# Streaming attention and a GELU layer in one kernel: weight transfers back to back, values of block 1 on SyncE, bias on block 0

## Chip, cores and metric

The kernel runs on one core of a Trainium2 chip. Its time is device microseconds; the number compared is the median of several executions. Beside it there is one profiled execution, from which the page and the trace come.

## What is computed

Four batches, eight heads, 768 tokens, head dimension 64. Attention with a causal window of 128 tokens and four sink tokens that are always seen; its output, put back to 3072 rows of 512, goes through x·w_in (512 by 2048), a quick GELU and ·w_out (2048 by 512).

```python
keep = is_sink | in_window                       # pos < 4, or 0 <= row - column < 128
scores = np.where(keep, scale * q @ k.T, -1e9)
a = exp(scores - max) / (sum + 1e-9)
x = (a @ v).transpose(0, 2, 1, 3).reshape(3072, 512)
h = x @ w_in
out = (h / (1 + exp(-1.702 * h))) @ w_out
```

## The kernel before

The work is cut into twelve blocks of 256 tokens (NK = 12; block k is batch k // 3, part r = k % 3), each with four pairs of heads. A block goes through these stages:

- **Load** (function `load`): q, k and v of the block in float32, on SyncE's DMA queue (SP); the first k is on ScalarE's. Blocks 0 to 3 load q and k in two halves each (KT = 4). In the kernel before, v of block 1 alone is loaded by GpSimd (POOL). Three buffers (RS) hold the float32 data.
- **Cast** to float16 (recorded at line 277, the line of a helper): on POOL, for the first two blocks on VectorE (DVE), ScalarE (ACT) and POOL, as the planner places them.
- **Turn**: q and k are transposed into blkT, by TensorE (PE, line 504, then a copy) for blocks 0 to 3, by DMA transposes on SP from block 4.
- **Scores** (function `scores`): matmuls (line 586) and exp on ACT (line 606). What the window hides is taken away in one of two ways. For k < KM, bias matmuls on PE (line 579: bias times identity, accumulated ahead of the scores) put a large negative number there before the exp. For k >= KM, a multiply by a 0/1 mask on DVE follows the exp (line 613). KM is 2 before.
- **Sinks** (line 544, exp at 552) for blocks with r > 0; then the product with v (line 646), the division (664, 666), and the transpose to xT (685 and 692 for the first three blocks, a DMA transpose on SP later).
- **mm1** (line 713): eight groups of 8 matmuls per block, each followed by tanh on ACT (725) and a multiply on DVE (727) into gT. At most three groups are open (RTH = 3). w_in is cut into chunks w0 to w3, each of which serves two groups.
- **mm2** (line 741): 32 matmuls of 512 columns per block, 16 for each of its two row tiles, with chunk w4 + s // 2 of the weights for group s; scaling on ACT (759), stores on SP (773).

mm1 of block k - 1 and mm2 of block k - 2 run among the attention work of block k. The weights arrive as eight transfers that cast to float16 on the way (function `weights`, line 348), all issued by POOL, whose instruction stream they share with the casts.

**What sets the order.** A planner written in the kernel (`Plan.run`) places every operation on an engine at a modelled time, with costs, ends and buffers; the instruction order on each engine is the order of these times. `o.end` of a DMA is its modelled landing. The 700 ns of SLACK are added for DMA transposes alone. All loads and weights are also put in one list by priority and each must be planned after the one before it (`behind`). On top of that, from the tenth on, each gets a real wait on an earlier transfer ("gates"): the one some 3.8 us of transfer ahead of it (4.5 for those that POOL issues), so that few transfers are in flight at once. The order of the list is a0, a1, w0, w1, w2, w3, w4, a2, w5, w6, w7, where a2 stands for q, k and v of block 2 and w4 is the first chunk of w_out.

Of the kernel before, what the change touches and what calls it, by code (L numbers as in the profile page):

```python
# [33 lines left out]
class Op:  # L34
    def __init__(self, engs, fn, deps, prio, acq, rel, kind):

        self.engs, self.fn = engs, fn
        self.deps = [d for d in dict.fromkeys(deps) if d is not None]
        self.prio, self.acq, self.rel, self.kind = prio, acq, rel, kind
        self.eng = self.start = self.end = self.banks = self.places = self.behind = None  # L40
        self.users = []


HOP = {
    ("PE", "ACT"): 60, ("PE", "DVE"): 60, ("ACT", "DVE"): 60, ("DVE", "PE"): 80, ("ACT", "PE"): 80,
    ("DVE", "ACT"): 60, ("POOL", "PE"): 100, ("POOL", "DVE"): 100,
}
RING, LANES, SLACK = 163, 8, 700
ENGINES = ("PE", "ACT", "DVE", "POOL", "SP")


class Plan:
# [4 lines left out]
    def op(self, eng, dur, lat, fn, deps=(), prio=0.0, acq=None, rel=(), kind=""):  # L57
        return self.any({eng: (dur, lat)}, lambda _: fn(), deps, prio, acq, rel, kind)
# [8 lines left out]
    def run(self, warm=None, warm_until=0.0, late_bank=0.0):  # L67
# [4 lines left out]
        free = {e: 0.0 for e in ENGINES}  # L72
# [12 lines left out]
        def after(d, e):  # L85
            if d.eng != e or isinstance(d.engs[e][1], tuple):
                return d.end + HOP.get((d.eng, e), 50)
            return d.start + d.engs[e][0] + (0 if d.eng == "PE" else 60)

        def could(o, e):  # L90

            if o.behind and o.behind.start is None:
                return None, None
            s = max([free[e]] + [after(d, e) for d in o.deps])
            line = landed[e == "POOL"]
            if isinstance(o.engs[e][1], tuple) and len(line) >= LANES:
                s = max(s, line[-LANES])
            if not o.acq:
                return s, s
            cls, n = o.acq  # L100
            times = sorted(bank_free.values())
            places = sorted(count[cls].values())
            if len(times) < n or len(places) < n:
                return s, None
            return s, max(s, times[n - 1], places[n - 1])

        while todo:
            best = None
            for e in ENGINES:
                found = sorted(  # L110
                    [(*could(o, e), o) for o in ready[e]], key=lambda x: (x[2].prio, x[2].seq)
                )
                keep, held_from = [], None
                for s0, s, o in found:
                    if s0 is None:
                        continue
                    if o.acq and o.acq[1] > 2 and (s is None or s > s0):

                        held_from = s0 if held_from is None else min(held_from, s0)
                        if s is not None:  # L120
                            keep.append((s, o))
                        continue
                    if s is None or (o.acq and held_from is not None and s >= held_from):
                        continue
                    keep.append((s, o))
                if not keep:
                    continue
                first = min(s for s, _ in keep)
                s, o = min(((s, o) for s, o in keep if s <= first + 20), key=lambda x: (x[1].prio, x[1].seq))
                lat = o.engs[e][1]  # L130
                key = s if len(o.engs) == 1 else s + lat - min(x[1] for x in o.engs.values())
                if best is None or key < best[0]:
                    best = (key, s, o, e)
            if best is None:
                raise RuntimeError("no operation can be planned")
            _, s, o, e = best
            dur, lat = o.engs[e]
            if e == "PE" and warm and s < warm_until:
                t = max(free["PE"], 400.0)
                while t + 110 < s:  # L140
                    order.append((t, -1, warm, e, None))
                    t += 60
            for x in o.engs:
                ready[x].remove(o)
            o.eng, o.start = e, s
            if o.acq:
                cls, n = o.acq
                o.banks, o.places = [], []
                for _ in range(n):
                    b = min((b for b in bank_free if bank_free[b] <= s), key=lambda b: (bank_free[b], b))  # L150
                    del bank_free[b]
                    o.banks.append(b)
                    p = min((p for p in count[cls] if count[cls][p] <= s), key=lambda p: (count[cls][p], p))
                    del count[cls][p]
                    o.places.append(p)
            free[e] = s + dur
            if isinstance(lat, tuple):
                ns, nd = lat
                t = s + dur
                while sum(n * min(1.0, (b - t) / max(b - a, 1.0)) for a, b, n in ring[e] if b > t) + nd > RING:  # L160
                    t += 25
                free[e] = t
                soft = e == "POOL"
                begin = max(s + (2200 if soft else 1300), dma_free[soft])
                shared = max(0.0, min(dma_free[not soft] - begin, ns))
                if shared:
                    dma_free[not soft] += shared
                dma_free[soft] = begin + ns + shared
                ring[e].append((begin, dma_free[soft], nd))
                landed[soft].append(dma_free[soft] + 900)  # L170
                o.end = dma_free[soft] + 900 + (SLACK if o.kind in ("turn", "xturn") else 0)
            else:
                o.end = s + lat
            for owner, i in o.rel:
                t = o.end + 80
                bank_free[owner.banks[i]] = t
                count[owner.acq[0]][owner.places[i]] = t
            for u in o.users:
                u.left -= 1
                if not u.left:  # L180
                    for x in u.engs:
                        ready[x].append(u)
            order.append((s, o.seq, o.fn, e, o))
            todo -= 1
# [9 lines left out]
def kernel(  # L194
# [11 lines left out]
    nc = tc.nc  # L206
# [11 lines left out]
    scale = float(1.0 / np.sqrt(Dh))  # L218
    PAIRED_FROM, RR = 2, 3
    KT, KX, AHEAD = globals().get('OPT',{}).get('KT',4), 3, globals().get('OPT',{}).get('AHEAD',0)  # L220
    RB, KM, HIDE = 4, globals().get('OPT',{}).get('KM',2), 60000.0
    RS, RQ, RV, RA, RX, RG, RTH, RO = 3, 2, 4, 6, 3, 5, 3, 3

    pool = ctx.enter_context(tc.tile_pool(name="sb", bufs=1))
# [116 lines left out]
    def weights(j, at):  # L341
        if j < 4:
            src = moe_w_in[:, bass.ts(j, 512)].rearrange("(c p) f -> p c f", p=P)
            to = w_in16[:, :, bass.ts(j, 512)]
        else:
            src = moe_w_out[bass.ts(j - 4, 512), :].rearrange("(c p) f -> p c f", p=P)
            to = w_out16[:, 4 * (j - 4) : 4 * (j - 4) + 4]
        o_w[j] = op("POOL", 780, (2800, 33), lambda: nc.gpsimd.dma_start(to, src), prio=at, kind="w")  # L348
        loads.append(o_w[j])

    L = OPT.get('L',17300.0)
# [2 lines left out]
    def load_at(x):  # L354
        return NEVER + 10 * LOADS.index(x) + 3 if x in LOADS else 10000.0 + (int(x[1:]) - 3) * L
# [17 lines left out]
    def load(k):  # L373
# [7 lines left out]
        for e, src in enumerate((q, k_ap)):  # L381
# [10 lines left out]
            else:  # L392
                def f(e=e, src=src, dma=dma):
                    return dma.dma_start(dst[:, e], src[b, :, t0 : t0 + TB].rearrange("h (p i) d -> p h i d", i=2))
                lq[e].append(op(eng, 450, (1850, 64), f, war, prio=prio + e / 2, kind="load"))
            loads.extend(lq[e])
            if k == 1:
                o_first.extend(lq[e])
        def lv(dma, h):
            return lambda: dma.dma_start(dv[:, h], v[b, h, t0 : t0 + TB].rearrange("h (p i) d -> p h i d", i=2))  # L400

        soft = k == 1
        o_lv = [op("POOL" if soft else "SP", 1000 if soft else 450, (1850, 64), lv(nc.gpsimd if soft else nc.sync, slice(0, 8)),
                   war, prio=load_at("w0") + 5 if soft else load_at("a1") + 1.5 if k == 0 else prio + 0.7, kind="load")]

        loads.append(o_lv[0])

        c16 = qk16[k % RQ]
# [391 lines left out]
    for a_, b_ in zip(loads, loads[1:]):  # L800
        b_.behind = a_
    for n, o in enumerate(loads):
        if 9 <= n < 4 + 5 * KT + 8:
            m, ahead = n - 1, 0.0
            while ahead < (4500 if "POOL" in o.engs else 3800):
                ahead += next(iter(loads[m].engs.values()))[1][0]
                m -= 1
            g = o_first[1] if o is o_w[0] else loads[m]
            o.deps.append(g)
            gates.append((o, g))  # L810

    warm_bank = bank[6]

    def warm(_):
        nc.tensor.matmul(warm_bank[:, 0:P], zero, zero, start=True, stop=True)  # L815

    order = plan.run(warm=warm, warm_until=12000.0, late_bank=12500.0)
    with tc.manual_schedule():
# [42 lines left out]
```

## Time and profile before

| | us |
|---|---|
| median of 5 runs | 227.02 |
| lowest and highest run | 226.24, 229.21 |
| profiled execution | 228.77 |
| span of its instructions | 226.8 |

Busy time and share of the span by engine: PE 218.6 us (96%), DVE 126.0 (56%), ACT 132.6 (58%), POOL 91.0 (40%). The mean granted clock of TensorE is 0.996 of full speed. HBM is read at 27.36 MB and written at 6.29 MB over the span.

All times inside the profile count from the start of the span. A timeline row gives start, duration, engine, line and operation, the operands and the count of instructions that are merged; in brackets stands the idle time of the engine just before it and what ended that. A row of the waits gives the total, the number and the longest wait. A row of the chain gives start and length of a piece. "DMA qk<-in_q_dram" is the load of q. In the rows on DMA queues, q1 is SP's, q10 ACT's, q0 POOL's; the numbers are packets, MB, and the time that the packets took as a share of 16 engines' span.

### The profile page before, as it was taken

The numbers are of one execution on the slowest core, as the hardware profiler recorded it, in microseconds if no ns is written. First come the engines' busy times: TensorE is split into PE (matmuls) and PEld (weight loads), VectorE is DVE, ScalarE is ACT, GpSimd is POOL, SyncE is SP. The second block draws the span as 40 slices with busy tenths as digits, with TensorE's granted clock in tenths as the row PEclk, the third lists the DMA queues.
The fourth block names the chain that finished last, engine by engine and source line by source line (L and its number), as shares of the span: only waits on it lengthen the run. The fifth ranks groups of instructions, "written<-read, shape, count | busy, mean of one in ns | idle before, by whom it ended". The sixth has DMA issues, their size and how long they took to land.

```text
span 226.8 us, 5442 instructions
## 1 busy us (share of the span) xinstructions
PE 218.6 (96%) x2170; PEld 153.4 (68%) x2170; DVE 126.0 (56%) x274; ACT 132.6 (58%) x262; POOL 91.0 (40%) x158
## 2 busy tenths in 40 slices
PE   8999989989999999999999999999999999999991
PEld 8968867576766766766766766766676676766640
DVE  1585856667744855665565655665555655633400
ACT  3298546576647865655576676565476476444310
POOL 8296056068993594906609709209200000000000
PEclk9999999999999999999999999999999999999998
DMA  5999999998978989599596786986812312230232
GB/s 189 317 197 169 221 242 160 289 288 240 269 142 163 259 165 260 122 188 285 111 230 176 140 211 160 142 208 165 165 24 47 65 30 46 65 71 5 49 74 64
DMA packets 64808, 36.36 MB, mean 160 GB/s; under 512 B 27760, under 2 KB 59520, under 8 KB 64784
## 3 DMA queue, kind: packets, MB, share of 16 engines
q1 hardware_dynamic: 60000, 30.55, 56.6%
q0 software_dynamic: 4416, 4.82, 13.3%
q10 hardware_dynamic: 368, 0.66, 1.0%
q8 instruction: 17, 0.28, 0.5%
q14 instruction: 7, 0.06, 0.1%
HBM read 27.36 MB, written 6.29 MB: 148 GB/s over the span
## 4 chain that ended last, share of the span: by engine, by line
PE 81%; DMA 12%; POOL 4%; DVE 1%; issue 0%; ACT 0%; POOLq 0%
PE bank L741 34%; PE bank L713 32%; PE bank L646 5%; DMA w_out<-in_moe_w_out_dram 5%; PE bank L586 4%; DMA w_in<-in_moe_w_in_dram 3%; PE bank L815 3%; DMA qk<-in_q_dram 3%; PE bank L544 1%; POOL qk L277 1%; POOL vs L452 1%; PE bank L504 1%; POOL w_out L348 1%; DVE blkT L277 0%; POOL v L400 0%
## 5 line engine op out<-in xcount | busy, mean ns | idle before, releaser
L713 PE MATMUL bank<-xT,w_in 128*128 128x256 f16 x768 | 101.3, 273 | 0.0
L741 PE MATMUL bank<-w_out,gT 128*128 128x512 f16 x384 | 99.6, 379 | 1.3 <-DMA w_out<-in_moe_w_out_dram 1.3
L727 DVE SCALAR_TENSOR_TENSOR gT<-th,bank 128x512 f16<-128x512 f16 x96 | 65.7, 684 | 44.9 <-ACT th L725 43.8
L713 PEld LDWEIGHTS <-w_in 128*128 128x128 f16 x768 | 72.4, 98 | 22.7 <-issue 2.7
L725 ACT ACTIVATE th<-bank 128x512 f16<-128x512 f32 x96 | 57.7, 601 | 44.5 <-PE bank L713 42.7
L277 POOL CAST qk<-qk 64x512 f16<-64x512 f32 (+1 forms) x72 | 43.9, 610 | 57.5 <-DMA qk<-in_q_dram 48.8
L606 ACT ACTIVATE at<-bank 128x512 f16<-128x512 f32 (+1 forms) x96 | 50.4, 571 | 14.9 <-PE bank L586 14.6
L741 PEld LDWEIGHTS <-gT 128*128 128x128 f16 x384 | 35.7, 98 | 24.9 <-issue 2.1
L613 DVE TENSOR_TENSOR at<-at,bank 128x1024 f16<-128x1024 f16 (+1 forms) x40 | 25.6, 639 | 20.8 <-ACT at L606 20.8
L277 POOL CAST v<-v 64x512 f16<-64x512 f32 x45 | 27.6, 612 | 3.4 <-DMA v<-in_v_dram 1.1
L646 PE MATMUL bank<-v,at 128*128 128x65 f16 x352 | 21.1, 193 | 0.2 <-DVE v L277 0.2
L759 ACT ACTIVATE osb<-bank 128x512 f32<-128x512 f32 (+1 forms) x24 | 14.2, 591 | 11.8 <-PE bank L741 11.8
L646 PEld LDWEIGHTS <-at 128*128 128x128 f16 x352 | 17.6, 97 | 3.7 <-issue 0.2
L552 ACT ACTIVATE ats<-bank 128x256 f16<-128x256 f32 x32 | 12.5, 391 | 7.9 <-PE bank L544 7.9
L666 DVE TENSOR_TENSOR xb<-bank,rcp 128x256 f16<-128x256 f32 x36 | 15.1, 421 | 0.5
L646 PE MATMUL bank<-vs,ats 128*128 128x65 f16 x128 | 14.8, 193 | 0.0
L664 DVE RECIPROCAL rcp<-bank 128x4 f32<-128x4 f32 x48 | 8.6, 179 | 10.3 <-PE bank L646 9.8
L586 PE MATMUL bank<-blkT 64*128 64x256 f16 x192 | 13.4, 244 | 0.0
L586 PEld LDWEIGHTS <-blkT 64*128 64x128 f16 x256 | 8.0, 94 | 7.7 <-issue 6.2
L646 PEld LDWEIGHTS <-ats 128*128 128x128 f16 x128 | 12.0, 97 | 1.9 <-ACT th L725 0.2
L815 PE MATMUL bank<-zero 128*128 128x128 f16 x99 | 8.9, 268 | 1.0 <-DVE zero L290 1.0
L277 ACT COPY blkT<-bank 128x512 f16<-128x512 f16 (+1 forms) x11 | 5.2, 501 | 7.1 <-PE bank L504 7.1
(42 smaller groups left out, 92.0 us busy)
## 6 DMA issues: line engine op xcount, KB each, us to landing
out_dram<-osb SPq DMA_DIRECT2D x47, 128.0 KB, 3.0
v<-in_v_dram SPq DMA_DIRECT2D x11, 512.0 KB, 6.8
qk<-in_q_dram SPq DMA_DIRECT2D x8, 512.0 KB, 4.6
qk<-in_k_dram SPq DMA_DIRECT2D x8, 512.0 KB, 5.6
qk<-in_q_dram SPq DMA_DIRECT2D x8, 256.0 KB, 6.2
w_in<-in_moe_w_in_dram POOLq DMA_DIRECT2D x4, 512.0 KB, 7.7
w_out<-in_moe_w_out_dram POOLq DMA_DIRECT2D x4, 512.0 KB, 8.7
qk<-in_k_dram SPq DMA_DIRECT2D x6, 256.0 KB, 5.8
```

What stands on the lines that cost most here:

```text
L277: {"POOL": nc.gpsimd.tensor_copy, "DVE": nc.vector.tensor_copy, "ACT": nc.scalar.copy}[e](out=out, in_=in_)
L586: nc.tensor.matmul(f32(o_s, 2 * n + i)[:, c : c + w], src[d, j], Q[d].rearrange("d j s -> d (j s)")[:, q0 : q0 + w], start=k >= KM, stop=T ...
L606: nc.scalar.activation(out=A[:, i, 0:W], in_=f32(o_s, 2 * n + i)[:, 0:W], func=AF.Exp, scale=scale)
L613: nc.vector.tensor_tensor(out=A[:, :, 0:W], in0=A[:, :, 0:W], in1=mask[:, c0 : c0 + W].unsqueeze(1).to_broadcast((P, 2, W)), op=ALU.mult,)
L646: nc.tensor.matmul(avp()[:, j, i], a_, v_, start=(n == 0), stop=(n == len(mms) - 1))
L666: o_n = op("DVE", 300, 425, lambda: nc.vector.tensor_tensor(out=X, in0=avp()[:, :, :, 0:D], in1=rc.to_broadcast((P, 2, 2, D)), op=ALU.mult ...
L713: nc.tensor.matmul(f32(holder[0])[:, bass.ts(e, TB)], w_in16[:, c, bass.ts(Fi, P)], X[:, c] if k < KX else X2[:, :, c], start=(c == 0), st ...
L725: o_t = op("ACT", 477, 600, lambda first=first: nc.scalar.activation(out=th[first.places[0]], in_=f32(first), func=AF.Tanh, scale=0.851), ...
L727: o_g[k, s] = op("DVE", 565, 690, lambda first=first, s=s: nc.vector.scalar_tensor_tensor(out=g[:, 2 * s : 2 * s + 2].rearrange("p a t -> ...
L741: nc.tensor.matmul(f32(holder[0]), g[:, Fi, bass.ts(j, P)], w_out16[:, Fi], start=(Fi == 0), stop=(Fi == NF - 1),)
L759: nc.scalar.mul(O[:, c], f32(holder[0])[:, c], 0.5)
L815: nc.tensor.matmul(warm_bank[:, 0:P], zero, zero, start=True, stop=True)
```

## The change

Six edits: the planner's SLACK is replaced by a lateness of each operation (`late`: 700 ns for transposes and weights, 2000 ns for loads of blocks 2 and up), and operations get an earliest time (`begin`); weights get such earliest times; the weights lose their gates except the first, which now waits for the last load of k of block 1 instead of its second load of q; v of block 1 is loaded by SP, right after v of block 0; KM is 1 instead of 2; the modelled transfer time of a weight is 2750 ns instead of 2800. The gates of the loads stay, by the same rule of 3.8 us.

```diff
-RING, LANES, SLACK = 163, 8, 700
+RING, LANES = 163, 8
...
-            s = max([free[e]] + [after(d, e) for d in o.deps])
+            s = max([free[e], o.begin] + [after(d, e) for d in o.deps])
...
-                o.end = dma_free[soft] + 900 + (SLACK if o.kind in ("turn", "xturn") else 0)
+                o.end = dma_free[soft] + 900 + o.late
...
-    RB, KM, HIDE = 4, globals().get('OPT',{}).get('KM',2), 60000.0
+    RB, KM, HIDE = 4, globals().get('OPT',{}).get('KM',1), 60000.0
...
-        o_w[j] = op("POOL", 780, (2800, 33), lambda: nc.gpsimd.dma_start(to, src), prio=at, kind="w")
+        o_w[j] = op("POOL", 780, (2750, 33), lambda: nc.gpsimd.dma_start(to, src), prio=at, kind="w")
+        o_w[j].begin = 9000.0 + 800 * j + (OPT.get('WS',3000) if j > 1 else 0)
...
+            for o in lq[e]:
+                o.begin = 1.0 if k > 1 else 0.0
...
-        soft = k == 1
-        o_lv = [op("POOL" if soft else "SP", 1000 if soft else 450, (1850, 64), lv(nc.gpsimd if soft else nc.sync, slice(0, 8)),
-                   war, prio=load_at("w0") + 5 if soft else load_at("a1") + 1.5 if k == 0 else prio + 0.7, kind="load")]
-
+        o_lv = [op("SP", 450, (1850, 64), lv(nc.sync, slice(0, 8)), war,
+                   prio=load_at("a1") + 1.5 + k / 8 if k < 2 else prio + 0.7, kind="load")]
+        o_lv[0].begin = 1.0 if k > 1 else 0.0
...
-        if 9 <= n < 4 + 5 * KT + 8:
+        if o is o_w[0]:
+            g = o_first[-1]
+        elif o.kind == "load" and 10 <= n < 4 + 5 * KT + 8:
             m, ahead = n - 1, 0.0
-            while ahead < (4500 if "POOL" in o.engs else 3800):
+            while ahead < 3800:
...
-            g = o_first[1] if o is o_w[0] else loads[m]
-            o.deps.append(g)
-            gates.append((o, g))
+            g = loads[m]
+        else:
+            continue
+        o.deps.append(g)
+        gates.append((o, g))
...
+    for o in plan.ops:
+        o.late = {"turn": 700.0, "xturn": 700.0, "w": OPT.get('LW',700.0)}.get(o.kind, 0.0)
+    for o in loads:
+        if o.kind == "load" and o.begin > 0:
+            o.late = OPT.get('LL',2000.0)
```

What comes out on the engines: POOL issues w0 and w1 together, later w2, w3 and w4 together, then w5, w6 and w7 together, with casts between; one cast of q of block 1 is on POOL instead of DVE; PE has 24 bias matmuls instead of 56, DVE four mask multiplies more; the transposes of block 2 on PE stand behind 16 more matmuls of mm1; some stores stand ahead of DMA transposes on SP.

## The prediction

> **What bounds the kernel now.** I read the page first: the share of engines, the chain, the groups. TensorE is busy 96% of the span and carries 81% of the chain. Busy time alone proves little (see the skill below), so I went on to the waits of PE, and then to its timeline of the first 60 us, to see where it is really held.
>
> ```profile
> PE 218.6 (96%) x2170; PEld 153.4 (68%) x2170; DVE 126.0 (56%) x274; ACT 132.6 (58%) x262; POOL 91.0 (40%) x158
> ...
> PE 81%; DMA 12%; POOL 4%; DVE 1%; issue 0%; ACT 0%; POOLq 0%
> ```
>
> ```profile
> PE bank L741 <- DMA w_out<-in_moe_w_out_dram: 1.3, 2, 1.0
> PE bank L815 <- DVE zero L290: 1.0, 1, 1.0
> PE bank L504 <- POOL qk L277: 0.8, 1, 0.8
> PE bank L646 <- DVE v L277: 0.2, 1, 0.2
> ```
>
> The timeline of PE says when: the second group of matmuls shown here is the transposes of block 2, the first and third use w_out chunks 0 and 3.
>
> ```profile
> 30.52 1.02 PE L741 MATMUL bank<-w_out,gT 128*128 128x512 f16 x4 [0.27 <-DMA w_out<-in_moe_w_out_dram]
> ...
> 32.78 0.62 PE L504 MATMUL bank<-perm,qk 128*128 128x128 f16 x8 [0.80 <-POOL qk L277]
> ...
> 45.95 1.02 PE L741 MATMUL bank<-w_out,gT 128*128 128x512 f16 x4 [1.02 <-DMA w_out<-in_moe_w_out_dram]
> ```
>
> So from 8.82 (first real transposes) to 46 us PE loses 0.27 + 0.80 + 1.02 = 2.09 us to late DMAs, and from 50 to 200 us nothing: the stage table has PE 50.00 of 50.00 in both 100 to 150 and 150 to 200. From 46 us the time is the count of matmuls. A gain must come from fewer matmuls or from these 2.09 us; the tail (last matmul to the end) is untouched. The chain in order of time gives the cause of the last wait: w_in chunk 2 (issued 15.73) releases SP's loads of block 2 at 23.47, their cast on POOL (30.81) stands between the w_out issues, and the last weight, issued 34.58, lands after 11.33 us.
>
> ```profile
> 15.73 7.73 DMA w_in<-in_moe_w_in_dram
> ...
> 23.47 7.19 DMA qk<-in_q_dram
> ...
> 30.81 0.61 POOL qk L277
> ...
> 34.58 11.33 DMA w_out<-in_moe_w_out_dram
> ```
>
> **What the Trainium skill says.** (1) Trainium Kernel Development and Optimization, section Performance Expectations: matmul busy time is a bad measure, as matmuls are pipelined. Agrees: eight bias matmuls are "busy" 0.61 us, but the next instruction starts 0.54 us after them. I count starts, not busy time. (2) DMA: Bandwidth & Descriptors, section SWDGE vs HWDGE vs iDMA: a cast during the transfer can only be issued from GpSimd, whose cores compute the descriptors. So the weights stay on POOL; the trace shows 0.75 us of POOL for each. (3) Same page, section Queues, rings and completion order: each DMA engine takes turns between the queues that have work, packet by packet. The trace agrees only in part. SP issued q of block 2 at 23.47, yet a window of 22 to 26.5 us has only packets of the POOL queue (q0); between 41.5 and 43.5 the two share evenly.
>
> ```profile
> q0 software_dynamic: 861, 0.86, 117.2%
> ```
>
> ```profile
> q0 software_dynamic: 200, 0.20, 58.6%
> q1 hardware_dynamic: 193, 0.37, 53.1%
> ```
>
> In the trace's packet records the first packets of SP loads follow an issue after 1.2 to 1.5 us when POOL's queue is empty, after 3.4 us (23.47 to 26.9) and 3.9 us (37.57 to 41.5) when it is full. This delay is what the change plays with.
>
> **The change part by part.** The order of instructions on the engines is known; only times are not.
>
> *Bias on block 0 only (KM 2 to 1).* PE loses 32 bias matmuls (56 to 24). The rows "L579 ... x8" start 0.54 us before the next L586 in each of the four pairs (15.22/15.76, 17.08/17.62, 18.35/18.89, 21.09/21.63): 4 x 0.54 = 2.16 us less. DVE gains four mask multiplies (L613 in before, 128x1024): the timeline at 40.46 has 0.69 each, 2.76 us. They come after 17.5 us, before the first gT (L727). Cover: DVE is busy 3.36, 3.46 and 4.09 us in the three 5 us stages from 15 to 30, so about 4 us are free, but not where they fall. Following the new DVE order by the old durations: xT of block 0 is complete at 19.8 (18.8 before), mask 4 waits for exp until 21.2, the first gT starts at 21.9 (20.99), the eighth ends at 29.7 (30.74), with a pitch of 0.6 in dense stretches. mm1 has three th places, so PE can't be more than three groups ahead of gT. At the eighth group PE is then about 1.0 us ahead, not 2.16: 1.2 us is lost there. Bounds: 0.5 (only the late xT) and 2.2 (all of it). I take 1.2. Later nothing is lost: DVE is 56% busy.
>
> *Values of block 1 from POOL to SP, cast of q to POOL.* POOL loses one DMA issue of 0.90 (11.57) and gains a cast of 0.61, in its gap of 2.48 before 8.41, where q of block 1 has just landed. SP issues v of block 1 right after that of block 0 (4.99 + 0.6), before any weight; v of block 1 lands by 12 to 13, its casts wait for POOL only. Queued behind it on SP is nothing until 23 us. Cost nothing; gain at most the 0.15 DVE wait at 14.65, not counted.
>
> *Weights.* w_in 0 now waits for the last k of block 1 and stands behind POOL's ks copies (end 11.62): issue 11.62 instead of 8.41, w_in 1 right after; then cast, vs copies (1.9), cast, and w_in 2, 3, w_out 0 at about 16.3 to 18.5, three v casts (to 20.5), w_out 1 to 3 by 22.8 (34.58 before). The POOL casts of v of block 1 end at 20.5; PE asks for them at about 21.3. Rate: between 20 and 22 us the POOL queue writes 202 GB/s alone, 0.524 MB a chunk: 2.6 us each; in the window 15 to 20, beside POOL's own work, 146 GB/s, 3.6 us. From a first packet at 13: w_in 0 at 16, w_in 1 at 18.7 to 20, w_in 2 at 21.3 to 22.8, w_in 3 at 23.8 to 25.3, w_out 0 at 26.5 to 28. PE asks for w_in 0 at 19.3, w_in 2 at 24.5, w_in 3 at 26, w_out 0 at 30: all in time, by under 1 us for w_in 3.
>
> SP's loads of block 2 wait for w_in 2 (q) and w_in 3 (k), as before, so they are issued at 21.3 to 22.8, but now with five weights in the queue. If the delay stays 3.4 to 3.9 us and they then take turns with the weights, one packet each (0.081 us a 1 KB weight packet, 0.085 a 2 KB load packet on each of 16 engines, from 202 GB/s in 20 to 22 us and 387 in 6 to 8 us), q takes 16 turns of 0.166 = 2.7 us: landed by 28 to 30.5, cast by 31.7. PE asks for it at 32.5 (the order puts 16 more mm1 matmuls, 1.7 us, ahead of these transposes). k the same 2.7 us later, against 35.2 on PE. v of block 2, in 512 B packets (0.025 us at 329 GB/s in 30 to 32 us): 64 turns of 0.105 = 6.7 us, landed by 39.7, cast by 42.3 at the latest, against 41.2. w_out 3 lands near 40, against 43.6.
>
> *Planner's late landing, SP and PE order.* Same instructions, moved. Some outs move ahead of a DMA transpose on SP; their osb is by the new PE order some 3 us earlier, so I see no new wait. The last 100 matmul groups are in the same order. Zero.
>
> **Sum.** Bias -2.16; waits that go -2.09; DVE +1.2; new waits for v of block 2, w_in 3 or q, bounded by 0 and 1.7 in this picture, +0.85. Total -2.2. The profiled execution took 228.77 us (span 226.8, 1.97 around it): span 224.6, execution 226.6. That execution lay 1.75 above the median 227.02; I take the 2.2 off the median: 224.8.
>
> **The rivals.**
> *A, slower: block 2's loads are held until the weights have drained.* Place: SP's q loads of block 2, PE's transposes behind them. For it: the empty window above; and in both cases seen the loads began when some 0.14 MB of weights were left in the queue, so "until it is nearly empty" fits as well as "a fixed delay". Against: the delay in both was near 3.5 us, and when they began the sharing was even. With eight chunks from 13 us the queue empties at 35.5 to 36; q lands at 37, second cast at 38.2; PE waits from 32.5 to 38.2 = 5.7 us. -3.05 + 5.7 = +2.65: 229.7. It decides from a q cast that ends after 35.5 (32.5 plus the 3.05 gained).
> *B, DVE becomes the pace of 17 to 30 us.* For: 2.76 us put in front of the first gT, in-order. The whole 2.16 is lost, and PE's later arrival means only the w_out 3 wait of 1.02 is saved: 226.0. Against: 4 us free by the stage table.
> *C, the loads come 1 to 2 us late.* The waits at 30.5 and 32.8 come back in other places, v of block 2 with them: -2.2 + 2 = 226.8.
> That the change doesn't do what it says is ruled out by the order: 32 matmuls go, POOL issues in twos and threes.
>
> **Numbers.** About 1% (2.3 us) is what a measurement of this kernel can tell from no change. Forecast 0.48 (own range 223.3 to 226.0; faster 0.38, same 0.10); B 0.14 (same 0.13, faster 0.01); C 0.12 (same 0.10, slower 0.02); A 0.26 (slower 0.24, same 0.02). Together faster 0.39, same 0.35, slower 0.26. The range: below, 2.16 + 2.09 less the lower bound of 0.5 for DVE: 3.75 off, 223.3; above, it takes in the lower half of A: 229.6.
>
> **What would show it.** Right: L579 x24, no PE wait on w_out, the w_out issues all before 23 us, the first packets of block 2's loads 3.5 to 4 us after their issue, transposes of block 2 near 32.5 with under 1 us of wait, last stage unchanged. Wrong: PE waits over 3 us for POOL's cast of block 2 (A); ACT waiting for DVE, or PE for gT, over 2 us between 18 and 30 (B); any PE idle after 60 us (the planner's order).

## The result, and the profile after

The changed kernel takes 229.05 us (median of 44 executions, 226.94 to 231.22), the kernel before in the same sitting 227.52 us (median of 79). The ratio is 1.0062, with a 95% interval of 1.0044 to 1.008: slower by 0.6%, some 1.4 us, where 2.2 us less had been forecast. The ratios leave out the few executions more than 1.5% above the fastest of their kernel; the medians have all of them. The profiled execution of the changed kernel has a span of 228.2 us, that of the kernel before 226.8.

The 44 executions fall into two groups by the clock that TensorE was granted on average: 21 have 0.993 or less and a median of 230.04 us, 23 have more and a median of 227.85. Of 83 executions of the kernel before that ran beside the experiments, 2 are of the first kind. The profiled execution of the changed kernel (0.993) belongs to it. One stretch of 3.41 us at half clock, as it is seen below, takes 0.0075 off the mean over 228 us, so a mean of 0.993 or less says that there was at least one.

The head of the page, engines and then the chain. As before, it looks like a full TensorE, with 32 matmuls fewer:

```profile
PE 218.9 (96%) x2138; PEld 152.3 (67%) x2138; DVE 126.9 (56%) x276; ACT 132.4 (58%) x263; POOL 90.8 (40%) x158
...
PE 82%; DMA 10%; POOL 4%; DVE 1%; SPq 0%; issue 0%; ACT 0%; POOLq 0%
```

The waits of PE (total, times, longest) tell more. Both waits for w_out and the wait for POOL's cast of q are gone; a new one, for the casts of v, is larger than all three:

```profile
PE bank L649 <- POOL v L278: 2.8, 2, 1.8
PE bank L822 <- DVE zero L291: 1.0, 1, 1.0
PE bank L688 <- DVE xn L669: 0.5, 2, 0.2
PE bank L649 <- DVE v L278: 0.2, 1, 0.2
```

The timeline of PE shows where. The rows are the first use of w_out 0, the transposes of block 2, and the first matmuls with v of block 2:

```profile
30.01 1.03 PE L744 MATMUL bank<-w_out,gT 128*128 128x512 f16 x4
...
32.62 0.61 PE L507 MATMUL bank<-perm,qk 128*128 128x128 f16 x8
...
41.27 0.20 PE L649 MATMUL bank<-v,at 128*128 128x65 f16 x1
43.27 0.19 PE L649 MATMUL bank<-v,at 128*128 128x65 f16 x1 [1.80 <-POOL v L278]
...
44.60 0.21 PE L649 MATMUL bank<-v,at 128*128 128x65 f16 x1 [0.99 <-POOL v L278]
```

w_out 0 and the transposes run without a wait. Then PE stands from 41.3 to 43.27 and from 43.5 to 44.6, 3.1 us from start to start. The chain in order of time gives the reason: v of block 2 is issued at 26.73 and is 15.15 us under way, and its first cast follows at once.

```profile
17.31 8.18 DMA w_in<-in_moe_w_in_dram
...
26.73 15.15 DMA v<-in_v_dram
...
41.94 0.62 POOL v L278
```

POOL was not late: its timeline has it waiting 6.63 us for that transfer, long after its last weight issue.

```profile
20.72 2.23 POOL L349 DMA_DIRECT2D w_out<-in_moe_w_out_dram  x3
...
31.15 0.61 POOL L278 CAST qk<-qk 128x512 f16<-128x512 f32 x1 [0.72 <-DMA qk<-in_q_dram]
...
34.69 0.61 POOL L278 CAST qk<-qk 128x512 f16<-128x512 f32 x1 [0.64 <-DMA qk<-in_k_dram]
41.94 2.61 POOL L278 CAST v<-v 64x512 f16<-64x512 f32 x4 [6.63 <-DMA v<-in_v_dram]
```

What the DMA queues did meanwhile: first the window 22 to 26.5 us, then 27 to 32, then 33 to 39 (packets, MB, share of 16 engines; q0 is POOL's, q1 SP's).

```profile
q0 software_dynamic: 896, 0.90, 122.3%
```

```profile
q0 software_dynamic: 485, 0.48, 59.3%
q1 hardware_dynamic: 459, 0.85, 51.8%
```

```profile
q0 software_dynamic: 852, 0.85, 83.4%
q1 hardware_dynamic: 843, 0.45, 35.5%
```

In both of the later windows the queues move the same number of packets. While q and k of block 2 are loaded (2 KB packets) SP's queue gets 0.85 of 1.33 MB by that; while v is (512 B packets), it gets 0.45 of 1.30 MB. v, with the smallest packets, is the transfer that one packet for one packet treats worst.

The last view is the stage table from 41.3 us on (columns: length, PE, PEld, DVE, ACT, POOL busy, granted clock, DMA share, GB/s). After the idle time the clock of TensorE is at half for 3.4 us, and PE, though busy throughout, does half the work:

```profile
41.30:44.60 3.30, 0.51 (x9) 0.32 (x8) 0.69 (x1) 0.38 (x2) 2.45 (x4) 0.98 1.09 343
44.60:46.00 1.40, 1.40 (x10) 0.56 (x11) 0.61 (x2) 0.00 (x0) 1.39 (x3) 0.50 1.13 293
46.00:47.00 1.00, 1.00 (x13) 0.50 (x8) 0.00 (x0) 0.60 (x2) 1.00 (x3) 0.50 0.36 89
47.00:48.00 1.00, 1.00 (x5) 0.50 (x4) 0.00 (x0) 1.00 (x4) 0.94 (x2) 0.57 0.03 7
48.00:50.00 2.00, 2.00 (x34) 1.55 (x33) 1.95 (x5) 1.45 (x3) 1.35 (x3) 1.00 0.00 0
```

From 60 to 200 us PE is busy without a gap in both kernels, and the end is the same 36 matmuls in 7.93 us. So the theory was: the change gives what it should up to 41 us, and loses it and more to v of block 2, which shares the DMA engines with w_out 1 to 3 (theory 1), and to the half clock behind that wait. Its rivals: the bias part costs (theory 2); the planner's order under assumed lateness costs (theory 3).

### The profile page after: what moved, and what is told of

Its sections match the earlier page's. It is cut to its first block, busy times and chain, and to the rows that moved or that the text cites. A ratio compares the mean times of both kernels' runs of the same rounds, so it can differ in the third digit from the quotient of the medians.

```text
span 228.2 us, 5373 instructions
## 1 busy us (share of the span) xinstructions
PE 218.9 (96%) x2138; PEld 152.3 (67%) x2138; DVE 126.9 (56%) x276; ACT 132.4 (58%) x263; POOL 90.8 (40%) x158
## 4 chain that ended last, share of the span: by engine, by line
PE 82%; DMA 10%; POOL 4%; DVE 1%; SPq 0%; issue 0%; ACT 0%; POOLq 0%
PE bank L744 35%; PE bank L716 32%; DMA v<-in_v_dram 7%; PE bank L649 5%; PE bank L589 4%; DMA w_in<-in_moe_w_in_dram 4%; PE bank L822 3%; POOL v L278 2%; PE bank L547 1%; POOL w_in L349 1%; POOL vs L455 1%; PE bank L507 1%; SPq L389 0%; DVE blkT L278 0%; PE bank L688 0%
## 5 line engine op out<-in xcount | busy, mean ns | idle before, releaser
L730 DVE SCALAR_TENSOR_TENSOR gT<-th,bank 128x512 f16<-128x512 f16 x96 | 65.5, 683 | 44.2 <-ACT th L728 43.5
L616 DVE TENSOR_TENSOR at<-at,bank 128x1024 f16<-128x1024 f16 (+1 forms) x44 | 28.3, 644 | 21.9 <-ACT at L609 21.8
L649 PE MATMUL bank<-v,at 128*128 128x65 f16 x352 | 21.7, 193 | 3.0 <-POOL v L278 2.8
L822 PEld LDWEIGHTS <-zero 128*128 128x128 f16 x99 | 8.5, 128 | 1.0 <-DVE zero L291 1.0
```

What stands on the lines that cost most here:

```text
L616: nc.vector.tensor_tensor(out=A[:, :, 0:W], in0=A[:, :, 0:W], in1=mask[:, c0 : c0 + W].unsqueeze(1).to_broadcast((P, 2, W)), op=ALU.mult,)
L649: nc.tensor.matmul(avp()[:, j, i], a_, v_, start=(n == 0), stop=(n == len(mms) - 1))
L730: o_g[k, s] = op("DVE", 565, 690, lambda first=first, s=s: nc.vector.scalar_tensor_tensor(out=g[:, 2 * s : 2 * s + 2].rearrange("p a t -> ...
```

## The experiments

The first real transposes start between 7.5 and 8.9 us in these profiles (8.82 before, 8.94 changed). Where a part of a microsecond matters, times are therefore taken from an issue or from these transposes. Every ratio below is to the kernel before, run beside the experiment, with its 95% interval in brackets.

### The last weight waits for v of block 2

```diff
+        elif o is o_w[7]:
+            g = o_v2[0]          # the load of v of block 2
```

> The changed kernel, but the last weight (w_out 3) is issued only when v of block 2 has landed. PE's and SP's orders are the same; on POOL one weight issue moves behind the first v cast's wait. Theory 1 (the loss is v of block 2, held back by the w_out transfers on the same DMA engines, and the half clock that follows the idle PE): 0.5 MB less beside it, 2.6 us at the 202 GB/s of the weights, so v lands near 39.3 instead of 41.88, its casts end near 41.9 instead of 44.55, PE waits under 0.7 us at L649 instead of 3.1, no half clock at 44 to 48; w_out 3 then lands near 44, which may cost up to 1 us. Sum -3.5 (from -4.7 to -2.5): about 225.5 us. Theory 2 (the four mask multiplies that the bias part puts on DVE cost the time, the v wait only takes up slack): at most 0.5 us faster, since DVE's work is untouched. Theory 3 (the planner's order under assumed late landing costs it): no difference, as the order on PE is untouched.

Measured: 231.88 us, ratio 1.0207 (1.017 to 1.0244): slower still, by about 3 us. The timeline of POOL and the waits of PE of this kernel:

```profile
38.18 0.75 POOL L349 DMA_DIRECT2D w_out<-in_moe_w_out_dram  x1 [3.66 <-DMA v<-in_v_dram]
38.91 2.64 POOL L278 CAST v<-v 64x512 f16<-64x512 f32 x4
```

```profile
PE bank L746 <- DMA w_out<-in_moe_w_out_dram: 3.6, 1, 3.6
...
PE bank L651 <- POOL v L278: 0.7, 1, 0.7
```

With one chunk less beside it v is 11.94 us under way instead of 15.15 (the chain below), and PE's wait for it is down to 0.7 us, as theory 1 said; theories 2 and 3 have no room for that. But the forecast for the whole was wrong, again by a landing that was priced too early. I had let w_out 3 land near 44, as if it were alone; k and v of block 3, issued by SP at 37.22 and 38.50, took turns with it, and it took 8.91 us:

```profile
25.95 11.94 DMA v<-in_v_dram
...
38.18 8.91 DMA w_out<-in_moe_w_out_dram
```

So the wait was not taken away but handed to another transfer.

### PE kept busy in the wait

```diff
+            if k == 2 and p == 0:
+                for _ in range(32):
+                    nc.tensor.matmul(f32(o_a)[:, 384:512], zero, zero, start=True, stop=True)
```

> The changed kernel with 32 matmuls of zeros, 128x128, into unused columns of the attention output's bank, put between the first and the second v matmul of block 2, where PE stands idle; the rest of the order is the same. Theory 1: v of block 2 lands at 41.9 as before and PE can't go on before 43.2, but PE works for 1.7 of those 2 us, so the clock does not fall: granted clock 1.0 from 44 to 48, 1.6 us faster than the changed kernel: 227.4. If the clock falls anyway, or falls on its own account: 0 to +0.3 us. Theories 2 and 3 say nothing of the clock: no difference, or the 1.7 us of matmuls on top.

Measured: 228.18 us, ratio 1.0026 (1.0008 to 1.0044). The 32 matmuls stand just ahead of the first ones with v of block 2. The timeline of PE and the stage table (here length, PE busy, granted clock, DMA share, GB/s):

```profile
41.54 1.95 PE L642 MATMUL bank<-zero 128*128 128x128 f16 x32
...
44.56 0.19 PE L652 MATMUL bank<-v,at 128*128 128x65 f16 x1 [0.82 <-POOL v L278]
```

```profile
44.00:45.00 1.00, 0.44 (x6) 1.00 0.70 190
45.00:46.00 1.00, 1.00 (x16) 1.00 1.07 301
46.00:47.00 1.00, 1.00 (x15) 1.00 0.27 67
```

PE goes on at 44.56 as before, v being as late as ever, but at full clock. None of the 22 executions has a mean clock of 0.993 or less. More work made the kernel faster: 0.9 us by the medians, not the 1.6 expected. The expectation was read from one profile that had the drop; the two groups above are 2.2 us apart (230.04 less 227.85), and 21 of 44 executions are in the slower one, which is 1.05 us on average. Half clock for 3.41 us can take at most 1.7 of these 2.2 us; the rest may be a longer wait in the same executions, which no run shows. What is left, 228.18, is near the 227.85 of the executions without the drop.

### The bias part alone, in the kernel before

```diff
+OPT = {'KM': 1}
```

> The kernel before with the bias part alone (bias on block 0 only; 32 bias matmuls fewer, four mask multiplies more on DVE); POOL's order is the same. Theory 1: PE reaches w_out 3 some 1 us earlier and waits for it so much longer, 2 instead of 1.02 us, as this transfer is issued at 34.6 whatever PE does: within 0.5 us of the kernel before, unless the longer wait brings a half clock (then +1.6). PE before that wait is about 1 us earlier (first use of w_out 3 asked at 43.9 instead of 44.9). Theory 2 (the bias part itself costs): slower by 1 to 2 us, with PE waiting for gT or xT between 18 and 30.

Measured: 227.47 us, ratio 0.9994 (0.9975 to 1.0014): no difference. Theory 2, 1 to 2 us slower, is out. The size of theory 1 is met, its mechanism is not: PE doesn't wait 2 us for w_out 3, because its order has moved. It has other, smaller waits (q 0.6, ACT's ats 0.5, v 0.4, w_in 0.3, w_out 0.2), which add up to 2.0 us, as much as the 2.1 of the kernel before. So these waits don't say where the 2.16 us of matmuls went; from the first real transposes to the last 36 matmuls the two profiles differ by 0.5 us only (204.8 against 205.3). The section on the prediction comes back to it.

### The changed kernel without assumed lateness

```diff
+OPT = {'LL': 0.0, 'LW': 0.0}
```

> The changed kernel with the planner's assumed late landing of loads and weights set to 0 (transposes and turns keep theirs). POOL's order is the same; PE's order and a few output stores on SP move. Theory 3 (the order under assumed lateness costs): faster by 1 us or more, with v of block 2 landing as before but PE having other work there. Theory 1: v of block 2 lands near 41.9 all the same, and with no lateness assumed PE's order asks for it at the same place or earlier, so the wait is as long or longer: 0 to 1.5 us slower than the changed kernel.

Measured: 230.85 us, ratio 1.0171 (1.0124 to 1.0218): slower than the changed kernel by 1.8 us by the medians and 2.5 by the ratios, more than the 1.5 that theory 1 allowed. Theory 3 is out; the assumption helps. The timeline and the stage table:

```profile
32.23 1.03 PE L509 MATMUL bank<-perm,qk 128*128 128x128 f16 x8 [2.52 <-POOL qk L280]
```

```profile
30.00:32.00 2.00, 0.00 (x0) 0.98 1.15 286
32.00:34.00 2.00, 1.77 (x13) 0.50 1.18 232
```

PE asks for q of block 2 near 29.7, waits 2.5 us, gets the half clock there, and later waits 1.0 us for v as well. The 1.7 us of mm1 that the lateness puts ahead of these transposes are what the forecast had leaned on for q.

### v of block 2 in the weights' queue

The load goes from SP to POOL, between w_out 1 and w_out 2; nothing else in the order moves.

```diff
+    v2, soft = o_v2[0]
+    gates[:] = [(o, g) for o, g in gates if o is not v2]
+    order = [x for x in order if x[0] is not v2]
+    at = [n for n, x in enumerate(order) if x[0] is o_w[5]][0] + 1
+    order.insert(at, (v2, lambda e: soft(), "POOL"))
```

> The changed kernel with the load of v of block 2 moved from SP to POOL, between the issues of w_out 1 and w_out 2, so that it stands in the weights' own queue ahead of two of them; PE's order is the same. Theory 1 (v of block 2 is late because it takes turns, packet by packet, with w_out 1 to 3): nothing but q and k of block 2 takes turns with it now; it lands by 34 to 37 instead of 41.9, the 3.1 us of PE idle at L649 and the half clock after it go, w_out 2 and 3 land about 2 us later than before, near 40 and 43, against 39.4 and about 43 on PE, which may cost up to 1.5 us. Sum -4.2 (3.1, and 1.1 as the mean of a half clock that only some executions have) to -2.7 against the changed kernel: 225 to 226.4, faster than the kernel before. A rival, that POOL's extra issue of 0.9 us and its wait cost as much: 228 or more. Theories 2 and 3 (bias, planner): within 0.5 us of the changed kernel.

Measured: 226.1 us, ratio 0.9945 (0.9921 to 0.9969): inside the forecast, and faster than the kernel before. The timeline of POOL, then that of PE:

```profile
21.05 0.92 POOL L404 DMA_DIRECT2D v<-in_v_dram  x1
...
35.15 0.61 POOL L278 CAST qk<-qk 128x512 f16<-128x512 f32 x1 [1.40 <-DMA qk<-in_k_dram]
35.78 2.61 POOL L278 CAST v<-v 64x512 f16<-64x512 f32 x4
```

```profile
35.82 0.62 PE L509 MATMUL bank<-perm,qk 128*128 128x128 f16 x8 [0.64 <-POOL qk L278]
```

v has landed before POOL is done with k at 35.76, some 6 us earlier than in the changed kernel. PE waits neither for it nor for w_out, and no execution has the low clock. What is late next is k of block 2, by 0.64 us. One caution: on POOL's queue the packet records show v in 128 packets of 4 KB instead of 1024 of 512 B, so this run changes the size of the packets together with the queue. The next one changes the size alone.

### v of block 2 in larger packets

```diff
+        def lv2(h):
+            return lambda: nc.sync.dma_start(
+                dv.rearrange("p h i d -> p (h i d)")[:, 512 * h : 512 * h + 512],
+                v[b, h::2, t0 : t0 + TB].rearrange("p (g i) d -> g p (i d)", i=8))
```

> The changed kernel, but v of block 2 is loaded on SP in 2 KB pieces, in the layout of q, as two transfers (so the values of block 2 stand in the wrong places); bytes, queue and time of issue are the same, 16 packets to a DMA engine instead of 64. If the queues take turns by packets: it needs 16 turns of about 0.24 us (what q and k showed) after k has landed at 34.6, so it lands near 38.5 to 39 instead of 41.9, the casts end by 41.6, PE waits under 0.5 us: 2.7 us faster than the changed kernel and 1.1 more with the clock: near 225.5. If they share by bytes, or v is late because the engines are full: it lands near 41.5 as before and the time is that of the changed kernel within 0.5 us.

Measured: 225.36 us, ratio 0.9903 (0.987 to 0.9937). The timeline of POOL:

```profile
35.29 0.61 POOL L278 CAST qk<-qk 128x512 f16<-128x512 f32 x1 [0.72 <-DMA qk<-in_k_dram]
38.27 2.61 POOL L278 CAST v<-v 64x512 f16<-64x512 f32 x4 [2.36 <-DMA v<-in_v_dram]
```

The same bytes, on the same queue, at the same place in SP's order, issued at 27.56, are there at 38.27: 10.7 us instead of 15.15, in packets of four times the size. Its first cast comes 3.0 us after the last cast of k has begun; in the changed kernel it was 7.25 us (34.69 to 41.94). PE's wait for POOL's casts of v is gone, and with it the low clock in all 6 executions. That is sharing by packets, not by bytes, and it rules out that v was late because the engines were full.

### The bias back on block 1, with and without the late v

```diff
+OPT = {'KM': 2}
```

In the changed kernel:

> The changed kernel with the bias on blocks 0 and 1 as before (32 bias matmuls more, four mask multiplies fewer); POOL and SP as in the changed kernel. Theory 1: PE comes about 1 us later to v of block 2, which lands at the same time, so its wait is 1 us shorter and the half clock rarer: 0 to 1 us faster than the changed kernel. Theory 2 (the bias part costs): faster by more than 1.5 us, with less PE idle between 18 and 30.

Measured: 228.09 us, ratio 1.0024 (0.9998 to 1.005), 0.9 us faster than the changed kernel. The waits for v are 2.0 us in all instead of 2.8, and 8 of 22 executions have the low clock instead of 21 of 44. As theory 1 said, PE that comes later waits less.

In the kernel with v in the weights' queue:

> The kernel with v of block 2 in the weights' queue, and the bias on blocks 0 and 1. With no late v behind it, the bias part shows its own price: by theory 1 the 32 matmuls (2.16) less what DVE's multiplies took back (1.2), so this is 1.0 us slower than the same kernel with the bias on block 0. If DVE takes back all of the 2.16: the same time; if PE comes to a late w_out 2 or 3 in both: the same time too, with the wait seen at L744.

Measured: 225.76 us, ratio 0.9917 (0.9892 to 0.9943), against 0.9945 with the bias on block 0 alone: not slower by 1.0, if anything faster. The first use of w_out 0, here and with the bias on block 0:

```profile
29.18 1.03 PE L747 MATMUL bank<-w_out,gT 128*128 128x512 f16 x4
```

```profile
29.60 1.03 PE L746 MATMUL bank<-w_out,gT 128*128 128x512 f16 x4
```

The first real transposes start at 7.48 and 8.53, so these are 21.70 and 21.07 us after them. The pair of the changed kernel gives the same: 21.69 (30.57 less 8.88) and 21.07 (30.01 less 8.94). The bias part is worth 0.62 us there, in both pairs. By the last run of 36 matmuls it is worth nothing: with the bias on block 0 PE has waited 0.64 us for k of block 2 meanwhile, with it on both blocks PE has no gap from 20 to 100 us. The expectation had named a late w_out 2 or 3 as the way to no gain; it was k.

## Why the prediction was wrong

**Issues up to 41 us: right; landings later than predicted, but covered.** The last weight was issued by 22.95 us (22.8 predicted). SP's first packets came at 26.91, 3.9 us after the issue at 22.99 (3.4 to 3.9). The transposes of block 2 stood at 32.62 without a wait (32.5), those of k at 35.36 (35.2). All three old waits, 2.09 us, are gone. PE reached v of block 2 at 41.25 (41.2). But q landed at 31.1 us (28 to 30.5 predicted) and k at 34.6 (by 33.2), 0.6 and 1.4 us too late, and only the slack ahead of their transposes hid it.

**Bias and DVE: somewhat too small a loss, and in another place.** The first gT started at 21.73 (21.9 predicted), the eighth ended at 30.2 (29.7). 2.16 us of matmuls brought 0.62 us, so 1.5 us were lost instead of 1.2, inside the bounds of 0.5 and 2.2. But the prediction had PE wait at gT, and up to 31 us no matmul of mm1 waits for it. What waits is the transposes of xn, the divided output of the attention, which DVE makes. These are the waits of PEld, TensorE's loading of weights, between 9 and 31 us, in the changed kernel and in the one with the bias back:

```profile
PEld L688 <- DVE xn L669: 1.7, 6, 0.5
```

```profile
PEld L690 <- DVE xn L671: 0.5, 2, 0.3
```

The difference, 1.2 us, is most of the 1.5; the rest is not put down to a wait in the trace.

**New waits: the step that failed.** This term was 0.85 with bounds of 0 and 1.7; PE's idle time at v was 3.1 us. The prediction had v of block 2 "landed by 39.7, cast by 42.3 at the latest"; it landed at 41.88 and its casts ended at 44.55. The turn itself was nearly right: 843 packets in 6 us are 140 packets a us and queue, on 16 engines one in 0.114 us, 0.105 predicted. What was wrong is that a mean over 16 engines was taken for the landing. In the trace's packet records 85% of the packets of v have ended by 39.28 us, 94% by 39.80, the last at 41.38, and q's packets of the next block already run from 39.68. Between 40.60 and 41.29 a packet of v starts every 0.114 us, one turn, as if a single engine were left. For q and k together it is the same: 85% by 32.32, the last at 34.25. So the last of the engines, not the mean, sets the landing, here by 1.6 to 2 us. Most of the delay is there when k ends: the 32 turns of q and k took 7.3 us up to the last packet, where 32 times 0.166 is 5.3, and 64 turns of 0.114 us from there lead to 41.5. That it is the same engine both times fits, but the records don't name it. The Trainium skill says why the last must count: DMA: Bandwidth & Descriptors, section Why a DMA increments its semaphore by 16 and not by 1, has the 16 engines finish independently, and only all 16 mean "landed". The same page, section Latency and other measured facts, calls two of the 16 usually slower; a short tail of few packets would fit that, but no run here shows it. Why some engine falls behind stays open.

**The clock: not in the sum at all.** TensorE: Matmul & The Clock Gate of the Trainium skill, sections Part 1: The HAM clock gate (the "warmup" mystery) and HAM oscillation — how this bites in real kernels, says that an idle window of some 3.4 us puts PE at half clock, and that the windows run freely. The trace agrees on the windows. In the clock records of all ten profiles every stretch between two changes of the clock is a whole multiple of 3.413 us: in the changed kernel full for 37.547 us (11 of them), then half for one, in the run in which the last weight waits half for two (6.827 us). It doesn't agree that a window must be idle throughout. The table cuts each profile into these windows; the last column has, of those before the last 36 matmuls, the one with the most time without a matmul, and the clock in the window after it.

| kernel | PE's waits by its profile | executions with 0.993 or less | most idle time in a window, clock after it |
|---|---|---|---|
| v in the weights' queue, bias back | none over 0.2 us | 0 of 12 | 0.22 us, full |
| bias part alone | 2.0 us, in pieces up to 0.5 | 0 of 22 | 0.54 us, full |
| v in the weights' queue | 0.64 us | 0 of 13 | 0.64 us, full |
| changed kernel, PE kept busy | 0.82 us at v | 0 of 22 | 0.82 us, full |
| v in larger packets | 0.84 us | 0 of 6 | 0.84 us, full |
| kernel before | 0.27, 0.80 and 1.02 us | 2 of 83 | 1.02 us, full |
| last weight waits | 0.7 and 3.6 us | 6 of 6 | 1.87 and then 1.75 us, half twice |
| changed kernel, bias back | 2.0 us | 8 of 22 | 2.05 us, half |
| no assumed lateness | 2.5 and 1.0 us | 6 of 6 | 2.30 us, half |
| changed kernel | 2.8 us | 21 of 44 | 2.64 us, half |

With the windows in which the matmuls of the kernel end, every window of these profiles with 2.05 us or more of idle PE is followed by half clock, and none with 1.02 us or less. Between 1.74 and 1.87 us both occur: the two of the run in which the last weight waits, and full clock after 1.86 us at the end of the changed kernel and after 1.74 at the end of that with v in the weights' queue. So it is the idle time within one window that counts, not the sum of the waits: 2.0 us in small pieces came with no low clock in 22 executions, 2.0 us in one place with it in 8 of 22. Why only in 8 is not shown; a window that ends in the middle of the wait would do it.

**The new sum.** The prediction stood at -3.05 before new waits. With 3.1 for v and 1.05 for the clock on average it gives +1.1; measured were +1.5 by the medians, +1.4 by the ratio. The profiles show it more closely. From the first matmul with v of block 2 to the first of the next such group the changed kernel takes 7.00 us (41.25 to 48.25), the kernel with v in the weights' queue 2.43 for the same matmuls (41.70 to 44.13): 4.57 us go to v and the clock in this execution. From the first real transposes to the start of the last 36 matmuls the profiles have 205.27 us before (214.09 less 8.82), 206.62 after (215.56 less 8.94) and 202.90 with v in the weights' queue (211.43 less 8.53). Without the 4.57 us the changed kernel would be 3.2 us ahead of the kernel before, near the 3.05 that the prediction had without new waits. In part that is luck, as the bias part brought 0.62 us and not the 0.96 that it had there. The kernel with v in the weights' queue is 2.4 us ahead of the kernel before in the profiles, but 1.25 us by the ratio: the profiled execution of before was a long one, which the forecast knew, but took its waits as typical.

**The rivals.** A, the nearest in time with 229.7, is not what happened: it asked for q's transposes to wait 5.7 us, and they didn't wait. SP's loads were delayed by 3.9 us, not until the weights had drained. B is right in part: DVE took more than half of what the bias part was to bring, though not at gT. C had the right resource, loads that are late by 1 to 2 us, and named v, but with no place for the loss: all three loads of block 2 were late, v by 2.2 us, and only v's lateness met PE, where the clock added to it. No idle time of PE after 60 us was seen, so the planner's order cost nothing; without its assumption q would have been late too.

## What to carry to other kernels

A set of transfers that is issued early shares the DMA engines packet by packet with every load that comes later, and here the load with the smallest packets paid most. Give each transfer its deadline, put those that compete into one queue in the order of the deadlines, and move an urgent load in large packets: v between w_out 1 and w_out 2 gave 226.1 us instead of 229.05, 0.55% less than the kernel before, and v in larger packets on its old queue 225.36, though in a kernel that puts the values of block 2 in the wrong places, so that only its time counts. Holding one transfer back only made it the late one. Take a landing from the last of the engines, not from the mean rate. Look at the waits of TensorE by place and not by their sum: some 2 us of idle time close together put the half clock behind them, 2.0 us in small pieces did not. A part that saves work ahead of a transfer which is late anyway is worth nothing.

## What the runs showed of the hardware that was not expected

Two queues share the 16 engines one packet for one packet whatever their sizes: 485 packets of POOL's queue (1 KB) to 459 with 2 KB on SP's side, 852 to 843 with 512 B. The engines don't finish together: the last packet of a 0.5 MB load ended 1.6 us after 94% of them. SP's first packets came 3.9 us after their issue behind POOL's full queue, and 1.2 us after it with POOL's queue empty (a store of the changed kernel, 49.98 to 51.17); but the first load of the kernel before took 2.5 us (0.74 to 3.21) with an empty queue too, so the full queue as the cause is not shown. The clock of TensorE changes in steps of 3.413 us; in the ten profiles each step with 2.05 us or more of idle PE was followed by one at half clock, none with up to 1.02 us was, and in between, from 1.74 to 1.87 us, both occurred. 32 matmuls of zeros in the wait kept all 22 executions above a mean clock of 0.993.
